# Start-up loads of a two-layer squared-ReLU kernel: x on one DMA queue, bias and first weights on the other

## Chip, cores and metric

The kernel runs on one core of a Trainium2 chip. The metric is the device time of one execution in microseconds: the median of three runs before the change is 290.73 us (290.58 to 290.94).

## What is computed

The reference is a dense layer, a squared ReLU and a second dense layer, all in bf16. x is 2048 rows of 576, the hidden width is 4608:

```python
h = jnp.einsum("bsd,df->bsf", x, w1) + b1
r = jnp.where(h > zero, h, zero)
h = r * r
out = jnp.einsum("bsf,fd->bsd", h, w2) + b2
```

## The kernel before

The 2048 rows are worked in four blocks of 512. For each block the first layer gives the hidden activations transposed (hidden column on the partition, row along the free dimension) in 36 groups of 128 hidden columns, the tile hT; the second layer then contracts over those groups. TensorE does the matmuls of both layers (L181, L183, L196, L198, L202 and L217 for the first, L253 and L272 for the second). ScalarE adds the bias and applies the ReLU as it reads a result out of PSUM (L169), VectorE squares it (L170).

Since 576 is four and a half times 128, the first layer has two forms. The first four groups of hidden columns (G = 4) use weights in full height: the tile w1n holds four chunks of 128 input rows by 512 columns, and w1n8 the last 64 input rows, once in each half of the partitions. The other 32 groups (`a_rows`) run as two matmuls of 64 rows side by side in the array, with weights from w1_h. These need each slice of the transposed x in both halves of the partitions, which VectorE makes with two copies, `dup_windows` (L115, L116).

**Blocks 1 to 3** of x are transposed by DMA (`load_xT`, on SyncE's queue). **Block 0**, with which the change has to do, is transposed on TensorE, and its start goes like this:

- Six matmuls of 512 columns and one of 256 on a constant keep TensorE busy first (WARM, L61 to L63).
- x comes in four tiles of 128 rows (`load_x`, L72; 144 KB each), w1n in four chunks (`load_w1n`, L76; 128 KB each). SyncE issues x tiles 0 and 2 and then w1 chunks 0 and 2; ScalarE issues x tiles 1 and 3 and then w1 chunks 1 and 3.
- ScalarE then runs a dummy activation (L97), ahead of which its table is loaded, and issues the load of the first bias into b1_rows (L98, 9 KB), a tile that VectorE clears first (L86). SyncE goes on with the two w1n8 loads (L79), fourteen w1_h loads (L82), the DMA transposes and all the rest.
- `a_full(0, "k_outer")` (from L213 on) issues, in this order on TensorE: the transposes of tiles 0 and 1, those of tiles 2 and 3 (five for each tile, L146), then for each chunk k four matmuls over the first 256 rows (`part(0, k)`, L217), four of chunk 0 over the other 256 rows, the transpose of the bias (L159), the twelve left of the other 256 rows, and the four 64-row matmuls with w1n8 (`pair`, L196 and L198). After those comes `a_rows` (L181, L183).
- `x_copies` brings the transposes out of PSUM for each half of the rows: VectorE copies three of the five slices (L151, L153), ScalarE two (L152). `dup_windows(0)` comes after both halves.

The order on each engine is that of the program for everything under `keep`. The loads all pass through two queues, SyncE's and ScalarE's; a load that waits holds whatever stands behind it on the engine that issues it.

Of the kernel before, what the change touches and what calls it, by code (L numbers as in the profile page):

```python
# [17 lines left out]
def kernel(  # L18
# [9 lines left out]
    nc = tc.nc  # L28
    keep = tc.keep_in_program_order
    P = 128  # L30
# [5 lines left out]
    NFT = F // P  # L36
    NC = D // H
    NK = NC // 2
# [6 lines left out]
    RT = SB // P  # L45
# [12 lines left out]

    wps = ps_h.tile([P, 512], FP32, name="wps", tag="ph")
    ones = nc.const_aps.tensor(1.0, [P, 512], BF16)  # L60
    WARM = [512] * 6 + [256]  # L61
    for i, n in enumerate(WARM):
        keep(nc.tensor.matmul(wps[:, 0:n], lhsT=ones[:, 0:P], rhs=ones[:, 0:n], start=True, stop=True))  # L63

# [6 lines left out]
    def load_x(eng, rt):  # L71
        keep(eng.dma_start(out=xs[:, rt, :], in_=x2[rt * P:(rt + 1) * P, :]))  # L72

    def load_w1n(eng, k0, k1):
        src = w1[k0 * P:k1 * P, 0:GW].rearrange("(k p) f -> p k f", p=P)
        keep(eng.dma_start(out=w1n[:, k0:k1, :], in_=src))  # L76
# [8 lines left out]
    b1_rows = const.tile([P, P], BF16, name="b1_rows")  # L85
    nc.vector.memset(b1_rows[:], 0.0)  # L86
    load_x(nc.sync, 0)
    load_x(nc.scalar, 1)
    load_x(nc.sync, 2)
    load_x(nc.scalar, 3)  # L90
    for k in range(NK):
        load_w1n(nc.sync if k % 2 == 0 else nc.scalar, k, k + 1)

    ident = const.tile([P, P], BF16, name="ident")
    make_identity(nc, ident[:])
    warm = const.tile([P, 1], FP32, name="warm")
    keep(nc.scalar.activation(out=warm[:], in_=nc.const_aps.tensor(0.0, [P, 1], FP32), func=ACT.Relu))  # L97
    keep(nc.scalar.dma_start(out=b1_rows[0:NFT, :], in_=b1.rearrange("(ft p) -> ft p", p=P)))  # L98
    for h in range(2):
        load_w1n8(nc.sync, h)  # L100

# [242 lines left out]
```

## Time and profile before

| what | value |
|---|---|
| median of three runs | 290.73 us |
| the profiled execution, its own time | 290.52 us |
| its span, first to last instruction | 288.7 us |
| TensorE busy in the span | 284.6 us (99%) |
| ScalarE, VectorE busy | 96.5 us, 78.6 us |
| first transpose of x on TensorE | 3.76 us |
| first matmul of the first layer (L217) | 5.41 us |
| first matmul of `a_rows` (L181) | 9.50 us |
| first of SyncE's and ScalarE's loads issued | 0.73 us |

Times inside the span count from its first instruction. The profiled execution is one run; 1.8 us of its own time lie around the span. PE is TensorE, PEld its weight loads, DVE VectorE, ACT ScalarE, POOL GpSimd, SP SyncE; ACTq and SPq are the parts of these engines that issue DMAs. A DMA is issued, moves its bytes as packets on 16 DMA engines that all queues share, and lands when its semaphore is complete. In the tables of groups, waits and chains a line such as L72 is the line of the kernel that issued the work, and what stands behind an arrow is what released a waiting engine.

### The profile page before, as it was taken

The numbers are of one execution on the slowest core, as the hardware profiler recorded it, in microseconds if no ns is written. First come the engines' busy times: TensorE is split into PE (matmuls) and PEld (weight loads), VectorE is DVE, ScalarE is ACT, GpSimd is POOL, SyncE is SP. The second block draws the span as 40 slices with busy tenths as digits, with TensorE's granted clock in tenths as the row PEclk, the third lists the DMA queues.
The fourth block names the chain that finished last, engine by engine and source line by source line (L and its number), as shares of the span: only waits on it lengthen the run. The fifth ranks groups of instructions, "written<-read, shape, count | busy, mean of one in ns | idle before, by whom it ended". The sixth has DMA issues, their size and how long they took to land.

```text
span 288.7 us, 4690 instructions
## 1 busy us (share of the span) xinstructions
PE 284.6 (99%) x2027; PEld 138.9 (48%) x2032; DVE 78.6 (27%) x177; ACT 96.5 (33%) x152; POOL 0.9 (0%) x7
## 2 busy tenths in 40 slices
PE   8999999999999999999999999999999999999996
PEld 5544444444444555555544444444444455555555
DVE  3444544444500200000025444444440001100001
ACT  3666666666500000000027666666670000000000
POOL 0000000000000000000000000000000000000000
PEclk9999999999999999999999999999999999999999
DMA  6999999600001100000000000000000110000000
GB/s 198 236 244 197 265 388 246 94 0 2 0 18 36 37 16 18 16 16 18 16 16 2 1 2 0 2 0 2 0 2 0 36 39 16 16 16 19 32 17 18
DMA packets 31573, 16.59 MB, mean 57 GB/s; under 512 B 15552, under 2 KB 31552, under 8 KB 31552
## 3 DMA queue, kind: packets, MB, share of 16 engines
q1 hardware_dynamic: 30928, 15.72, 22.3%
q10 hardware_dynamic: 624, 0.57, 0.7%
q8 instruction: 16, 0.26, 0.4%
q14 instruction: 5, 0.04, 0.0%
HBM read 11.43 MB, written 2.36 MB: 48 GB/s over the span
## 4 chain that ended last, share of the span: by engine, by line
PE 97%; DMA 1%; SPq 0%; issue 0%; DVE 0%
PE ph L181 42%; PE po L272 38%; PE pt L253 11%; PE pn L202 4%; DMA w1n<-in_w_dram 1%; PE pn L217 1%; PE ph L183 1%; PE pn L196 1%; SPq L72 0%; DVE o_sb L274 0%; PE b1T_ps L159 0%; PE pn L198 0%
## 5 line engine op out<-in xcount | busy, mean ns | idle before, releaser
L181 PE MATMUL ph<-xTw,w_h 64*128 64x512 bf16 x576 | 124.6, 376 | 0.0
L183 PE MATMUL ph<-xTw,w_h 64*128 64x512 bf16 x576 | 124.6, 376 | 0.0
L272 PE MATMUL po<-w_sb,hT 128*128 128x448 bf16 (+2 forms) x612 | 109.4, 341 | 0.0
L169 ACT ACTIVATE r<-ph,b1T 128x512 bf16<-128x512 f32 x128 | 81.1, 685 | 41.6 <-PE ph L183 41.6
L181 PEld LDWEIGHTS <-w_h 64*128 64x128 bf16 x576 | 54.1, 94 | 68.3
L272 PEld LDWEIGHTS <-hT 128*128 128x128 bf16 x612 | 58.5, 98 | 51.0
L170 DVE TENSOR_TENSOR hT<-r 128x512 bf16<-128x512 bf16 x144 | 61.2, 426 | 76.9 <-ACT r L169 76.9
L183 PEld LDWEIGHTS <-w_h 64*128 64x128 bf16 x576 | 54.1, 94 | 0.0
L274 DVE TENSOR_TENSOR o_sb<-po,b_bc 128x448 bf16<-128x448 f32 (+2 forms) x17 | 10.2, 597 | 125.8 <-PE po L272 125.8
L253 PE MATMUL pt<-hT,w_sb 128*128 128x512 bf16 x142 | 31.3, 379 | 0.1
L169 ACT ACTIVATE r<-pn,b1T 128x512 bf16<-128x512 f32 x16 | 10.3, 688 | 62.0 <-PE pn L198 60.6
L253 PEld LDWEIGHTS <-w_sb 128*128 128x128 bf16 x144 | 14.1, 98 | 17.0
L256 ACT ACTIVATE oT<-pt,b2T 128x512 bf16<-128x512 f32 x4 | 2.7, 687 | 28.3 <-PE pt L253 28.3
L202 PE MATMUL pn<-xTw,w1n 128*128 128x512 bf16 x45 | 10.4, 379 | 0.4 <-issue 0.3
L202 PEld LDWEIGHTS <-w1n 128*128 128x128 bf16 x48 | 4.5, 98 | 6.0 <-issue 0.8
L217 PE MATMUL pn<-xTw,w1n 128*128 128x256 bf16 x32 | 3.7, 273 | 0.1
L63 PE MATMUL wps<-const-bfloat16-1.0 128*128 128x512 bf16 (+1 forms) x7 | 2.9, 597 | 0.8 <-PEq L328 0.8
L217 PEld LDWEIGHTS <-w1n 128*128 128x128 bf16 x32 | 3.0, 98 | 0.6 <-DMA w1n<-in_w_dram 0.3
L115 DVE COPY xTw<-xTw 64x2048 bf16<-64x2048 bf16 x4 | 2.8, 690 | 0.6 <-ACT xTw L152 0.5
L116 DVE COPY xTw<-xTw 64x2048 bf16<-64x2048 bf16 x4 | 2.8, 688 | 0.1
L196 PE MATMUL pn<-xTw,w1n 64*128 64x512 bf16 x8 | 2.4, 379 | 0.0
L198 PE MATMUL pn<-xTw,w1n 64*128 64x512 bf16 x8 | 2.4, 379 | 0.0
(21 smaller groups left out, 10.5 us busy)
## 6 DMA issues: line engine op xcount, KB each, us to landing
w_sb<-in_w_dram SPq DMA_DIRECT2D x2, 2592.0 KB, 15.2
w_h<-in_w_dram SPq DMA_DIRECT2D x14, 288.0 KB, 6.6
out_dram<-o_sb SPq DMA_DIRECT2D x15, 112.0 KB, 1.7
w_h<-in_w_dram SPq DMA_DIRECT2D x4, 144.0 KB, 3.2
out_dram<-ot SPq DMA_DIRECT2D x4, 128.0 KB, 2.0
x_sb<-in_x_dram ACTq DMA_DIRECT2D x2, 144.0 KB, 3.0
x_sb<-in_x_dram SPq DMA_DIRECT2D x2, 144.0 KB, 3.0
w1n<-in_w_dram ACTq DMA_DIRECT2D x2, 128.0 KB, 3.6
```

Of the source, the lines that this page charges most:

```text
L63: keep(nc.tensor.matmul(wps[:, 0:n], lhsT=ones[:, 0:P], rhs=ones[:, 0:n], start=True, stop=True))
L115: keep(nc.vector.tensor_copy(out=xT[0:H, SPC:SPC + 4, :], in_=xT[H:P, E3:E3 + 4, :]))
L169: keep(nc.scalar.activation(out=r[:], in_=bank[:], func=ACT.Relu, bias=b1T[:, ft:ft + 1], scale=1.0))
L170: keep(nc.vector.tensor_tensor(out=hTs[sb][:, ft, :], in0=r[:], in1=r[:], op=ALU.mult))
L181: keep(nc.tensor.matmul(bx[:], lhsT=w1_h[0:H, LO_C[i], jc], rhs=xT[0:H, LO_W[i], :], start=(i == 0), stop=(i == NC - 1)))
L183: keep(nc.tensor.matmul(by[:], lhsT=w1_h[H:P, UP_C[i], jc], rhs=xT[H:P, UP_W[i], :], start=(i == 0), stop=(i == NC - 1)))
L196: keep(nc.tensor.matmul(banks[2 * i][:], lhsT=w1n8[0:H, 2 * i * P:(2 * i + 1) * P], rhs=xT[0:H, SPC, :], start=start, stop=stop, skip_grou ...
L202: keep(nc.tensor.matmul(banks[g][:], lhsT=w1n[:, k, g * P:(g + 1) * P], rhs=xT[:, O + k, :], start=start, stop=stop))
L217: keep(nc.tensor.matmul(banks[g][:, hc], lhsT=w1n[:, k, g * P:(g + 1) * P], rhs=xT[:, O + k, hc], start=(h == 0 and k == 0), stop=False, s ...
L253: keep(nc.tensor.matmul(pt[:], lhsT=w2_sb[:, ft, DM:D], rhs=hT[:, ft, :], start=(i == 0), stop=(i == NFT - 1)))
L272: keep(nc.tensor.matmul(po[:, 0:d1 - d0], lhsT=hT[:, ft, jj * P:(jj + 1) * P], rhs=w2_sb[:, ft, d0:d1], start=(i == 0), stop=(i == NFT - 1)))
L274: keep(nc.vector.tensor_tensor(out=o_sb[:, d0:d1], in0=po[:, 0:d1 - d0], in1=b2_bc[:, d0:d1], op=ALU.add))
```

## The change

The warm-up has one matmul of 512 columns less. SyncE issues all four x tiles, in order, ahead of its other loads. ScalarE issues the bias first, then the four w1 chunks, and then has the dummy activation. Nothing else is edited; SyncE's later loads follow the x tiles directly.

```diff
-    WARM = [512] * 6 + [256]
+    WARM = [512] * 5 + [256]
...
     load_x(nc.sync, 0)
-    load_x(nc.scalar, 1)
-    load_x(nc.sync, 2)
-    load_x(nc.scalar, 3)
-    for k in range(NK):
-        load_w1n(nc.sync if k % 2 == 0 else nc.scalar, k, k + 1)
+    keep(nc.scalar.dma_start(out=b1_rows[0:NFT, :], in_=b1.rearrange("(ft p) -> ft p", p=P)))
+    for rt in range(1, RT):
+        load_x(nc.sync, rt)
+        load_w1n(nc.scalar, rt - 1, rt)
+    load_w1n(nc.scalar, NK - 1, NK)
...
     keep(nc.scalar.activation(out=warm[:], in_=nc.const_aps.tensor(0.0, [P, 1], FP32), func=ACT.Relu))
-    keep(nc.scalar.dma_start(out=b1_rows[0:NFT, :], in_=b1.rearrange("(ft p) -> ft p", p=P)))
     for h in range(2):
         load_w1n8(nc.sync, h)
```

## The prediction

> **What bounds the kernel now.** First the page: engine shares and the chain of work that ended last.
>
> ```profile
> span 288.7 us, 4690 instructions
> PE 284.6 (99%) x2027; PEld 138.9 (48%) x2032; DVE 78.6 (27%) x177; ACT 96.5 (33%) x152; POOL 0.9 (0%) x7
> PE 97%; DMA 1%; SPq 0%; issue 0%; DVE 0%
> ```
>
> TensorE works without a pause from its first real matmul to the end, so an edit ahead of that matmul is worth just the shift of it. The chain in order of time (start, length, what), first 12 us, shows what that is:
>
> ```profile
> 0.73 0.40 SPq L72
> ...
> 1.20 0.44 SPq L72
> ...
> 1.68 3.68 DMA w1n<-in_w_dram
> 5.36 0.05 issue
> 5.41 2.36 PE pn L217 x20
> ```
>
> Call the start of the first L217 matmul T0: 5.41 us. It waits for w1 chunk 0, third on SyncE's queue (issued 1.68, landed 5.36). The timeline of weight loads shows what is ahead of it (start, busy, line, idle time before):
>
> ```profile
> 2.44 0.15 PEld L63 LDWEIGHTS <-const-bfloat16-1.0 128*128 128x128 bf16 x1 [0.27 <-issue]
> 2.86 0.15 PEld L63 LDWEIGHTS <-const-bfloat16-1.0 128*128 128x128 bf16 x1 [0.28 <-issue]
> 3.76 0.56 PEld L146 LDWEIGHTS <-x_sb 128*128 128x128 bf16 x10 [0.75 <-DMA x_sb<-in_x_dram]
> 4.55 0.56 PEld L146 LDWEIGHTS <-x_sb 128*128 128x128 bf16 x10 [0.23 <-DMA x_sb<-in_x_dram]
> 5.40 2.08 PEld L217 LDWEIGHTS <-w1n 128*128 128x128 bf16 x20 [0.29 <-DMA w1n<-in_w_dram]
> ```
>
> Ten transposes (tiles 0 and 1) start at 3.76, ten (2 and 3) at 4.55, done by 5.11; then 0.29 us idle. In program order all 20 stand ahead of T0. Last the windows (busy time of each engine, clock, DMA share, GB/s):
>
> ```profile
> 1.90:2.70 0.80, 0.80 (x3) 0.30 (x2) 0.00 (x0) 0.09 (x1) 0.00 (x0) 1.00 0.96 255
> 2.70:3.70 1.00, 1.00 (x3) 0.15 (x1) 0.00 (x0) 1.00 (x1) 0.00 (x0) 1.00 1.06 332
> 3.70:5.30 1.60, 1.47 (x21) 1.12 (x20) 0.77 (x4) 0.39 (x2) 0.00 (x0) 1.00 1.00 335
> ```
>
> The sixteen DMA engines are full from 1.9 to 5.3 us. T0 is set by how many bytes move ahead of the last thing that TensorE needs, whichever queue issues them.
>
> **What the skill says.** (1) DMA: Bandwidth & Descriptors, section Issuing engines are not separate DMA queues: both queues run on the same 16 engines. The trace agrees: 255 to 335 GB/s at a share of 1. (2) The same page, section Queues, rings and completion order: each engine goes round-robin between queues by packet. The packet records agree: while both queues are loaded, each starts about half the packets (3.0 to 5.0 us: 302 and 316). (3) TensorE: Matmul & The Clock Gate, section What's actually happening: the array is at half clock until it was busy for a free-running window of about 3.4 us. Agrees: warm-up loads are 427 ns apart for 512 columns, transposes 56 ns for 128, and the clock record grants full speed at 3.66 us for 286.72 us, 84 windows of 3.413.
>
> **Part 1, one warm-up matmul of 512 fewer.** Loads at 2.44 and 2.86 are 0.427 us apart, so TensorE is free at 3.28 rather than 3.71 us. By itself it saves nothing: tile 0 lands at 3.72. What it risks is the clock: the grant at 3.66 comes with TensorE busy for 2.9 of the 3.41 us before it; without the matmul and before any transpose it is 2.5. Whether that is enough the trace doesn't show; rival B prices it. Lower bound nothing.
>
> **Part 2, x alone on SyncE's queue, in order.** Landings here are an issue's start plus its time to landing in the DMA view. Today tiles 0 and 1 share the engines and land at 3.72 and 3.53, tiles 2 and 3 at 4.51 and 4.34. After: SyncE issues them 0.47 us apart (0.73 and 1.20 in the chain), at about 0.73, 1.20, 1.66, 2.13. First bytes move at 1.92, as today. ScalarE now issues the bias first; its bytes are nothing (9 KB), but its issue takes 0.70 us and waits for the memset (ends 0.94), so w1 chunk 0 is issued at about 1.71 and its bytes, 1.03 us later by ScalarE's first load of today, at 2.75. Until then x is alone: 0.84 us x 255 GB/s = 214 of 590 KB. The rest, 376 KB, shares with w1: a turn is 1152 against 1024 bytes, 53% of 334 GB/s = 177 GB/s, 2.12 us, to 4.87. From the last x packet today (4.05) to its landing (4.51) is 0.46 us, so tile 3 lands at about 5.33, 0.8 later than x is complete today. Check: 2.13 plus the 3.2 us that an x load of the second turn takes today is 5.33. Tiles 0 to 2 come at about 3.2, 3.8 and 4.6; their transposes are hidden under the wait for tile 3.
>
> After that landing come 0.04 us of release and five transposes, 0.28: T0 = 5.65, against 5.41: **+0.25 us**. The bounds: if x kept all the bandwidth that it is issued for, tile 3 lands 2.5 us after issue (the lowest lag of a load in this stage, a w1n8 one of 64 KB), at 4.6, and T0 is 4.95 (-0.45); if ScalarE's queue weighed as today, tile 3 lands like the fourth load of SyncE's queue today, 2.16 + 3.9 = 6.06, and T0 is 6.4 (+1.0). I take +0.25: the first ignores the full engines, the second ScalarE's later start, worth some 0.5 us of that.
>
> **Part 3, w1 chunks on ScalarE's queue.** Chunk 0: 131 KB at 157 GB/s from 2.75, landed near 4.1, 1.5 us ahead of use. Chunks 1 and 2, issued at 2.19 and 2.68, land near 5.0 and 5.8; used at T0 + 0.44 and T0 + 0.87 (20 matmuls take 2.18 us by load starts), 6.09 and 6.52. Chunk 3 is a ninth load, and the trace shows what a ninth does today:
>
> ```profile
> SPq L79 <- DMA x_sb<-in_x_dram: 0.9, 1, 0.9
> ```
>
> Eight semaphores are used in turn, and the ninth load waits until the first user of its semaphore has landed. Chunk 3 then goes out when tile 0 or the bias is in, 3.2 to 3.9 us, and lands near 6.2 to 6.9; needed at T0 + 1.31 = 6.96. Cost nothing, at the far end close to it.
>
> Queued behind that wait on ScalarE: the table load (1.28 us, today 2.61 to 3.89), the dummy activation (0.20) and the L152 copies, today 5.33 to 6.41, held up by the bias issue at 4.59. After: 3.2 + 0.45 + 1.28 + 0.20 puts L152 at 5.2 to 5.9; its first use is at 6.52 and it takes 0.59: hidden. The second copy ends near 6.5 to 7.1, the two window copies (1.4 us) at 7.9 to 8.5, and their user starts at T0 + 3.65 = 9.3: hidden. The bias is today transposed at 7.49 without a wait; earlier gains nothing.
>
> **Part 4, what SyncE issues next.** The two w1n8 loads and then 14 w1_h loads follow x on SyncE; today the first goes out at 3.54. Their wait becomes the bias's landing (near 3.2) or tile 1's (3.8): the stream shifts by -0.3 to +0.3 us. The tightest user today is the third row group: its load lands at 12.98, TensorE takes it at 13.18. With T0 0.25 later that slack is 0.4: no stall, but a gain over some 0.2 to 0.5 us would be given back there.
>
> **Sum.** 0 + 0.25 + 0 + 0. The profiled execution took 290.52 us, of which 1.8 lie around the span; 290.52 + 0.25 = 290.8. It is 0.21 under the median of the runs, 290.73, so on the median 291.0 (+0.09%). I count a change of 0.2% (0.58 us) as what a measurement of this kernel tells from none.
>
> **Rivals.** A, likeliest: as summed, 291.0, with 290.7 to 291.4 for the landing of tile 3 at 5.0 to 5.7.
>
> B, **the clock comes a window late**, the slower side. Place: the grant at 3.66. Price: it moves to 3.66 + 3.41 = 7.08; tile 3's five transposes take 107 rather than 56 ns (+0.26), and from T0 = 5.9 to 7.08 the L217 matmuls go at half speed, losing 0.6. With the 0.25: +1.1, 291.8. It decides if 2.5 us of warm-up with the transposes after it are too little for the window, or if transposes count for less than matmuls. For it: the busy part is cut from 85% to some 73%, and nothing shows the limit. Against: tile 0 lands at 3.2, so its five half-speed transposes fill 3.3 to 3.8 and the window to about 82%.
>
> C, **x gets through early**: the 4.95 of part 2, held by the third row group to about 0.4: 290.3. For it: x has a head start of 0.84 us. Against: full DMA engines.
>
> D, nothing moves: w1 chunk 0 would have to stay last. It lands near 4.1, so that needs tile 3 at 5.1; A's range has it.
>
> **Chances.** A 0.52, B 0.31, C 0.12, 0.05 for a later stream of w1_h loads or tile 3 at 6 us (291.5 and up). Slower by over 0.2% (above 291.3): B nearly whole, 0.29, a tenth of A, 0.05, and 0.05, together 0.39. Faster (under 290.15): 0.05 out of C. Same: 0.56. The range, 290.3 to 292.0, leaves out a third of C, the top of B and half of the last case, about 0.13; A's own is 290.7 to 291.4.
>
> **What would show it.** Right: the idle time before T0 is put down to x rather than w1; the last five L146 loads stand alone near 5.4; w1 chunk 0 lands a microsecond early; T0 is 5.5 to 5.8; later groups shift by the same amount. B shows as L217 loads twice as far apart as today's 109 ns, up to 7.1 us. C shows as T0 under 5.2 and a wait of L183 for a w1_h load. Wrong altogether: x3 landing under 4.8, or a wait for w1 chunk 3 or for L152 amid the L217 matmuls.

## The result, and the profile after

| | before | after |
|---|---|---|
| median of six runs, us | 290.67 (290.30 to 290.94) | 293.40 (291.66 to 293.93) |
| ratio, 95% interval | | 1.0087 (1.0060 to 1.0113) |
| the profiled execution, its own time and span, us | 290.52, 288.7 | 292.95, 291.2 |
| weight load of the first L217 matmul (L216 after), us | 5.40 | 6.60 |
| first matmul of `a_rows` in the chain, us | 9.67 | 12.08 |

The change makes the kernel 0.87% slower, some 2.5 us, where 0.25 us were predicted and 1.1 us in the worst rival. None of the versions that were run, with one of its edits or with several, came out faster than the kernel before. Lines after L98 stand one lower in the changed kernel: L145 is the transposes, L216 the first matmuls, L180 `a_rows`.

The page of the changed kernel, engine shares:

```profile
span 291.2 us, 4692 instructions
PE 286.6 (98%) x2031; PEld 140.2 (48%) x2031; DVE 78.5 (27%) x177; ACT 96.3 (33%) x152; POOL 0.9 (0%) x7
```

TensorE is busy 2.0 us more than before, with one warm-up matmul less to do, so a part of the loss is not idle time but slower work. The chain in order of time (start, length, what):

```profile
1.65 3.79 DMA x_sb<-in_x_dram
5.44 0.05 issue
5.49 1.42 PE tb L145 x10
6.91 3.27 PE pn L216 x20
10.18 0.06 PE b1T_ps L158
```

Before, the chain ran over w1 chunk 0 and its landing at 5.36. Now it runs over x tile 2, issued at 1.65 and landed at 5.44, and over the transposes of tiles 2 and 3. The first twenty L216 matmuls take 3.27 us; they took 2.36. The timeline of weight loads (start, busy, line, idle before) shows the rest:

```profile
3.01 1.07 PEld L145 LDWEIGHTS <-x_sb 128*128 128x128 bf16 x10 [0.43 <-DMA x_sb<-in_x_dram]
5.49 0.45 PEld L145 LDWEIGHTS <-x_sb 128*128 128x128 bf16 x5 [1.41 <-DMA x_sb<-in_x_dram]
6.19 0.45 PEld L145 LDWEIGHTS <-x_sb 128*128 128x128 bf16 x5 [0.26 <-DMA x_sb<-in_x_dram]
6.60 2.86 PEld L216 LDWEIGHTS <-w1n 128*128 128x128 bf16 x16
```

Tiles 0 and 1 come early, as was wanted (2.97 and 3.53). Tile 2 then lets TensorE idle from 4.08 to 5.49, and tile 3 comes at 6.15. The view ends at 9.4 us, and the sixteen L216 loads up to there take 2.86 us, where all twenty took 2.08: TensorE is still at half clock for most of them (the clock record grants full speed at 9.00). The windows of DMA traffic, in the stretches that the prediction used (the last two columns are the share of the DMA engines and GB/s):

```profile
1.90:2.70 0.80, 0.80 (x3) 0.30 (x2) 0.00 (x0) 0.00 (x0) 0.00 (x0) 1.00 0.96 287
2.70:3.70 1.00, 1.00 (x8) 0.66 (x7) 0.00 (x0) 0.21 (x1) 0.00 (x0) 1.00 0.89 196
3.70:5.30 1.60, 0.64 (x7) 0.38 (x4) 0.69 (x3) 1.59 (x3) 0.00 (x0) 1.00 0.96 310
```

Before it was 255, 332 and 335. The DMA engines move 196 GB/s from 2.7 to 3.7 us at a share of 0.89: they are held by slow packets, not out of work. In the packet records of that microsecond nine of 203 packets took 0.33 to 0.84 us, a third of all packet time, beside the usual 0.05; the kernel before has two such among 333.

The shift of 2.4 us adds up by steps. Tile 3's landing replaces chunk 0's as the last thing needed: 6.15 against 5.36, 0.79. Its transposes then lie on the path: five take 0.41 at half clock (6.19 to 6.60), 0.28 of it at any clock and 0.13 for the clock. From there to the transpose of the bias the loads take 3.31 us instead of 2.09, 1.22 for the clock. The sum is 2.42; the first `a_rows` matmul is 2.41 late.

### The profile page after: what moved, and what is told of

It is laid out like the page before. It is cut to its first block, busy times and chain, and to the rows that moved or that the text cites. A ratio compares the mean times of both kernels' runs of the same rounds, so it can differ in the third digit from the quotient of the medians.

```text
span 291.2 us, 4692 instructions
## 1 busy us (share of the span) xinstructions
PE 286.6 (98%) x2031; PEld 140.2 (48%) x2031; DVE 78.5 (27%) x177; ACT 96.3 (33%) x152; POOL 0.9 (0%) x7
## 3 DMA queue, kind: packets, MB, share of 16 engines
HBM read 11.43 MB, written 2.36 MB: 47 GB/s over the span
## 4 chain that ended last, share of the span: by engine, by line
PE 97%; DMA 1%; SPq 0%; DVE 0%; issue 0%
PE ph L180 42%; PE po L271 37%; PE pt L252 11%; PE pn L201 4%; PE pn L216 2%; DMA x_sb<-in_x_dram 1%; PE ph L182 1%; PE pn L195 1%; PE tb L145 0%; SPq L72 0%; DVE o_sb L273 0%; PE b1T_ps L158 0%; PE pn L197 0%
## 5 line engine op out<-in xcount | busy, mean ns | idle before, releaser
L180 PE MATMUL ph<-xTw,w_h 64*128 64x512 bf16 x576 | 124.6, 376 | 0.0
L180 PEld LDWEIGHTS <-w_h 64*128 64x128 bf16 x576 | 54.1, 94 | 68.3
L201 PEld LDWEIGHTS <-w1n 128*128 128x128 bf16 x48 | 4.5, 98 | 6.0 <-issue 0.8
L216 PE MATMUL pn<-xTw,w1n 128*128 128x256 bf16 x32 | 4.8, 322 | 0.0
L216 PEld LDWEIGHTS <-w1n 128*128 128x128 bf16 x32 | 3.7, 118 | 0.9
L145 PE MATMUL tb<-ident,x_sb 128*128 128x128 bf16 x20 | 2.7, 311 | 1.1 <-DMA x_sb<-in_x_dram 1.1
L145 PEld LDWEIGHTS <-x_sb 128*128 128x128 bf16 x20 | 1.9, 139 | 2.1 <-DMA x_sb<-in_x_dram 2.1
```

Source lines behind the costliest of these rows:

```text
L145: keep(nc.tensor.transpose(tb[h][bank][:, slot, q * P:(q + 1) * P], xs[:, j, c0:c0 + P], ident[:]))
L180: keep(nc.tensor.matmul(bx[:], lhsT=w1_h[0:H, LO_C[i], jc], rhs=xT[0:H, LO_W[i], :], start=(i == 0), stop=(i == NC - 1)))
L201: keep(nc.tensor.matmul(banks[g][:], lhsT=w1n[:, k, g * P:(g + 1) * P], rhs=xT[:, O + k, :], start=start, stop=stop))
L216: keep(nc.tensor.matmul(banks[g][:, hc], lhsT=w1n[:, k, g * P:(g + 1) * P], rhs=xT[:, O + k, hc], start=(h == 0 and k == 0), stop=False, s ...
```

## The experiments

Each run is compared with the kernel before on the same chip; a ratio is given with its 95% interval. Each also has one profile, and a landing or a rate read from it is one sample: in three profiles below with the same loads (changed kernel, old warm-up, hole filled) tile 3 lands at 6.15, 6.53 and 6.88.

### The clock

Theory L puts the whole loss down to the loads: x tile 3 lands late, and nothing else is lost. Two theories add a late clock for the slower L216 matmuls: W, the missing warm-up matmul makes it late; H, the hole on TensorE between the transposes of tile 1 and tile 2 does, with any warm-up.

**The short warm-up alone**, on the kernel before:

```diff
-    WARM = [512] * 6 + [256]
+    WARM = [512] * 5 + [256]
```

> The kernel before with one warm-up matmul of 512 less, its loads unchanged. Theory L (loads: the time comes from x tile 3 landing later because it shares the DMA engines with w1): no change, 290.7. Theory W (the shorter warm-up itself makes the full clock come late): slower, 291.5 to 292.5, with L217 loads twice as far apart for a while. Theory H (the clock is late because TensorE idles between the transposes of tile 1 and tile 2): the hole here is some 0.5 us between 3.3 and 3.8 only, so 290.7 to 291.0.

Measured: 291.07, ratio 1.0001 (0.9992 to 1.0010).

```profile
3.62 1.83 PEld L146 LDWEIGHTS <-x_sb 128*128 128x128 bf16 x20 [1.03 <-DMA x_sb<-in_x_dram]
5.40 2.12 PEld L217 LDWEIGHTS <-w1n 128*128 128x128 bf16 x20
```

All twenty transposes run without a hole between them, partly at half clock (the grant comes at 5.15). They end after w1 chunk 0 has landed (5.24), so the matmuls follow without idle time, at 5.40 as before and at full clock. W falls for this kernel.

**The new loads with the old warm-up**: the changed kernel with WARM as before.

```diff
-    WARM = [512] * 5 + [256]
+    WARM = [512] * 6 + [256]
```

> The changed kernel with the old warm-up (six of 512 and one of 256): the new loads alone. L: tile 3 lands near 6.1 again, first L217 matmul at 6.4 to 6.6, +1.1, and 291.8 if the clock comes in time. W: the clock comes in time, 291.8. H: the warm-up ends at 3.7, the transposes of tiles 0 and 1 at 4.8, a hole of 0.7 us is left before tile 2, so the clock is still late in a part of the runs: 292.3 to 293.2.

Measured: 293.44, ratio 1.0070 (1.0051 to 1.0090). Tile 3 lands at 6.53, the clock record grants full speed at 9.65. The new loads alone make most of the loss. Whether the missing warm-up matmul adds to it (1.0087 with it) can't be told, since the two intervals overlap. H, which asks for a hole (here 1.21 us), stands.

**The hole filled**, on the changed kernel:

```diff
                 for j in range(2):
                     x_transpose(j)
+                for _ in range(3):
+                    keep(nc.tensor.matmul(fill[:], lhsT=ones[:, 0:P], rhs=ones[:, 0:512], start=True, stop=True))
                 x_copies(0)
```

> The changed kernel with three matmuls of 512 on the constant between the transposes of tile 1 and those of tile 2, where TensorE idled from 4.0 to 5.5; the warm-up stays short. They are 1.28 us at half clock, 0.65 at full. L: 291.8 (tile 3 is as late as before, nothing else is lost). H: the clock comes within one window, so what was lost to it goes: 291.6 to 292.2, and the runs lie closer together. W: the clock is as late as in the changed kernel, 293.0 to 293.5.

Measured: 292.13 (291.84 to 292.34), ratio 1.0037 (1.0025 to 1.0049). The weight loads of its profile:

```profile
3.00 1.08 PEld L146 LDWEIGHTS <-x_sb 128*128 128x128 bf16 x10 [0.42 <-DMA x_sb<-in_x_dram]
4.04 0.25 PEld L224 LDWEIGHTS <-const-bfloat16-1.0 128*128 128x128 bf16 x2
4.57 0.15 PEld L224 LDWEIGHTS <-const-bfloat16-1.0 128*128 128x128 bf16 x1 [0.28 <-issue]
5.95 0.45 PEld L146 LDWEIGHTS <-x_sb 128*128 128x128 bf16 x5 [1.24 <-DMA x_sb<-in_x_dram]
6.93 0.28 PEld L146 LDWEIGHTS <-x_sb 128*128 128x128 bf16 x5 [0.52 <-DMA x_sb<-in_x_dram]
7.17 2.12 PEld L217 LDWEIGHTS <-w1n 128*128 128x128 bf16 x20
```

x is even later here than in the changed kernel (tile 3 lands at 6.88), but the grant comes at 6.63 and the twenty L217 loads take 2.12. Three matmuls that compute nothing win back over half of the loss: 1.0087 against 1.0037 of their own baselines, some 1.4 us. That part is the clock's, through the hole. The rest, 0.37% or 1.1 us, goes with the loads. It fits that two of the six runs with the old warm-up lie at 292.13 and 292.21, where the filled kernel is, and the other four at 293.44 to 293.79.

**A hole without new loads**: on the kernel before.

```diff
-    WARM = [512] * 6 + [256]
+    WARM = [512] * 2
```

> The kernel before with two warm-up matmuls instead of seven, so that TensorE idles from 1.8 to 3.5 us; loads unchanged, x lands at 3.7 to 4.5 and w1 chunk 0 at 5.3. It measures the clock alone. H (full clock comes only at the end of a window in which TensorE was busy for more than some three quarters): the clock comes between 6 and 8.5 us instead of 3.4 to 5.2, the first L217 matmul starts at 5.4 to 5.7, and the time is 0.5 to 1.2 us over the kernel before, 291.3 to 292.0. If the clock has no part in it: 290.8.

Measured: 291.74 (291.15 to 292.64), ratio 1.0030 (1.0020 to 1.0039). Its weight loads:

```profile
3.50 2.05 PEld L146 LDWEIGHTS <-x_sb 128*128 128x128 bf16 x20 [2.61 <-DMA x_sb<-in_x_dram]
5.50 3.11 PEld L217 LDWEIGHTS <-w1n 128*128 128x128 bf16 x20
```

The matmuls start 0.10 late and then take 1.03 us longer (3.11 against 2.08); the grant is at 7.53. With x and w1 landing as before, the late clock alone costs 0.9 us.

The records give the rule behind it. Full speed lasts a whole number of spans of 3.413 us in every profile that has the record (84 in the one before, 83 in the one after), so grants fall on a grid; its place against the kernel's start differs between executions (the grid passes 0.25 us before, 2.17 after). In the changed kernel the spans ahead of the grant were:

```profile
2.17:5.59 3.42, 2.27 (x16) 1.29 (x14) 0.69 (x3) 1.96 (x3) 0.00 (x0) 1.00 0.96 284
5.59:9.00 3.41, 3.41 (x21) 2.52 (x21) 2.06 (x5) 0.58 (x1) 0.00 (x0) 1.00 0.70 178
```

A span with TensorE busy for 2.27 us brought no grant, the next one, full, did. Over these profiles, every span that ended in a grant had 2.65 us or more busy, and the spans before them that brought none had up to 2.79 (with the bias last, below). The two overlap, so the busy time of the profile doesn't sort them alone. If there is one limit, it lies near four fifths of the span; that transposes count for less would explain the overlap (the 2.65 us, with w1 chunks 1 and 3 held back, are all warm-up, the 2.79 in part transposes), but it was not tested.

### The loads

Theory S was sharing of the DMA engines between x and w1, theory B a slow stretch made by the early bias. Both had to be changed on the way.

**One queue, in order**, on the changed kernel:

```diff
     for rt in range(1, RT):
         load_x(nc.sync, rt)
-        load_w1n(nc.scalar, rt - 1, rt)
-    load_w1n(nc.scalar, NK - 1, NK)
+    for k in range(NK):
+        load_w1n(nc.sync, k, k + 1)
```

> The changed kernel with the four w1 chunks on SyncE's queue behind the four x tiles; ScalarE issues the bias alone. L: x shares with nothing, tile 3 lands near 4.3 and w1 chunk 0 near 4.9, so the first L217 matmul is at 4.7 to 5.1, earlier than before; TensorE has no long hole and the clock is in time. But SyncE issues its w1n8 and w1_h loads some 1 us later than before, so L182 waits for w1_h: 290.6 to 291.6. If x is late for another reason than sharing (the bias ahead, or the order), tile 3 lands at 5.5 or later and the time is 292 to 293.

Measured: 291.38, ratio 1.0017 (1.0010 to 1.0023). Tile 3 lands at 4.90 and chunk 0 at 5.54; the matmuls start at 5.58. x without a rival lands 1.2 us earlier than in the changed kernel, which speaks for S, but 0.6 us later than the 4.3 expected. One queue alone moves less than two did before (321 and 334 GB/s in these two microseconds):

```profile
2.80:3.80 1.00, 1.00 (x9) 0.69 (x8) 0.00 (x0) 0.29 (x2) 0.00 (x0) 1.00 0.87 216
3.80:4.80 1.00, 0.79 (x9) 0.52 (x7) 0.63 (x3) 0.42 (x1) 0.00 (x0) 1.00 1.00 282
```

The expected wait for w1_h isn't seen; what waits is L216, for the chunks themselves.

**The bias last**, on the changed kernel:

```diff
-    keep(nc.scalar.dma_start(out=b1_rows[0:NFT, :], in_=b1.rearrange("(ft p) -> ft p", p=P)))
...
     keep(nc.scalar.activation(out=warm[:], in_=nc.const_aps.tensor(0.0, [P, 1], FP32), func=ACT.Relu))
+    keep(nc.scalar.dma_start(out=b1_rows[0:NFT, :], in_=b1.rearrange("(ft p) -> ft p", p=P)))
```

> The changed kernel with the bias load put back behind the dummy activation; x on SyncE's queue, w1 on ScalarE's, short warm-up. Theory S (sharing: x tile 3 is late because each queue gets half of the DMA engines): w1 chunk 0 now starts with x, 1 us earlier than in the changed kernel, so x shares from the start and tile 3 lands at 5.5 to 6.2; 292.0 to 293.5. Theory B (the early bias load is what slows the transfers between 2.8 and 4.3 us, where the changed kernel moves 138 to 254 GB/s and the one before 290 to 330): the rate in that stretch is back at 290 or more, tile 3 lands at 5.3 or earlier, and the time is 291.0 to 292.0.

Measured: 293.19, ratio 1.0079 (1.0056 to 1.0101). The rate is back, 365 and 348 GB/s in the two windows of 1 us from 2.8 on, and yet tile 3 lands at 6.45, since w1 shares from the first byte. The slow stretch and sharing are two things, and sharing from the first byte is enough for a late tile 3.

**The bias first**, on the kernel before (its load moved ahead of ScalarE's x tile 1):

```diff
     load_x(nc.sync, 0)
+    keep(nc.scalar.dma_start(out=b1_rows[0:NFT, :], in_=b1.rearrange("(ft p) -> ft p", p=P)))
     load_x(nc.scalar, 1)
...
-    keep(nc.scalar.dma_start(out=b1_rows[0:NFT, :], in_=b1.rearrange("(ft p) -> ft p", p=P)))
```

> The kernel before with the bias load put first on ScalarE's queue, ahead of x tiles 1 and 3; nothing else changed. B: the rate between 2.8 and 4.3 us falls to 140 to 260 GB/s here too, x tiles land over 1 us later, 292 or more. S: the rate stays near 300; x tiles 1 and 3 come 0.7 us later for ScalarE's later issue, x lands by 4.7 and w1 chunk 0 by 5.3, so 290.7 to 291.2.

Measured: 291.94 (290.92 to 293.57), ratio 1.0046 (1.0025 to 1.0066). The profile, of the slowest of the eleven runs, has 239 GB/s from 2.8 to 4.8 where the kernel before has 327; tile 3 lands at 6.53. The order "bias first" hurts without any of the other edits. B seemed shown.

**Two kernels that hold w1 back behind the table load.** The first is the changed kernel with all four w1 loads moved behind the dummy activation, the second the kernel before with chunks 1 and 3 there, ahead of the bias.

```diff
-        load_w1n(nc.scalar, rt - 1, rt)
-    load_w1n(nc.scalar, NK - 1, NK)
...
     keep(nc.scalar.activation(out=warm[:], in_=nc.const_aps.tensor(0.0, [P, 1], FP32), func=ACT.Relu))
+    for k in range(NK):
+        load_w1n(nc.scalar, k, k + 1)
```

```diff
-    for k in range(NK):
-        load_w1n(nc.sync if k % 2 == 0 else nc.scalar, k, k + 1)
+    for k in (0, 2):
+        load_w1n(nc.sync, k, k + 1)
...
     keep(nc.scalar.activation(out=warm[:], in_=nc.const_aps.tensor(0.0, [P, 1], FP32), func=ACT.Relu))
+    for k in (1, 3):
+        load_w1n(nc.scalar, k, k + 1)
```

> The changed kernel with the four w1 chunks put behind ScalarE's table load and dummy activation, so that they are issued some 1.4 us later and x has the DMA engines nearly to itself; bias first, short warm-up. S: tile 3 lands at 4.3 to 4.9 as in the run with one queue in order; the first L217 matmul waits for w1 chunk 0 instead, at 5.1 to 5.6; clock in time; 290.6 to 291.2. B: the slow stretch is still there and tile 3 lands at 5.5 or later; 292 or more.

> The kernel before with ScalarE's two w1 chunks (1 and 3) and its bias put behind its table load and dummy activation; x split over both queues, long warm-up. w1 chunk 0 is then alone behind x and lands at 4.8 to 5.0 instead of 5.36, so the first L217 matmul waits for the transposes, at 5.1; SyncE's w1n8 and w1_h loads come earlier too. By S 0.2 to 0.3 faster than the kernel before, 290.5 to 290.7; if chunk 1 comes too late for its use or the clock goes late, 290.9 to 291.2.

Measured: 292.41, ratio 1.0058 (1.0046 to 1.0071), and 291.03, ratio 1.0004 (0.9997 to 1.0011). Neither did what it was made for: the table load didn't hold ScalarE's next DMA, and the first chunk was issued at 1.68 and 1.73 while the table was loading. In the first kernel the other three were then held, one by one, by the semaphores of x tiles 0 to 2 (issued at 2.94, 3.99 and 4.99), and ScalarE's first copy behind them started at 5.37; it is the cost that the prediction feared for chunk 3 and that the changed kernel, whose chunk 3 goes out at 3.10, doesn't have. Tile 3 lands at 5.24 there, and the last first-layer matmuls of block 0 wait for the last w1 chunk, landed at 8.79. The second kernel has 365 GB/s from 2.8 to 4.3 us, without gain in time.

**The bias second**, between x tiles 1 and 3, on the kernel before:

```diff
     load_x(nc.scalar, 1)
+    keep(nc.scalar.dma_start(out=b1_rows[0:NFT, :], in_=b1.rearrange("(ft p) -> ft p", p=P)))
     load_x(nc.sync, 2)
```

> The kernel before with the bias load second on ScalarE's queue, between x tiles 1 and 3: both queues start at once as before, but the bias is still early. Theory B1 (the early bias load itself makes the transfers slow): between 2.8 and 4.3 us the rate falls to 140 to 280 GB/s and packets of over 250 ns are many, x tile 3 lands at 5.5 or later, 291.5 or more. Theory B2 (what is slow is a start with one queue only, because ScalarE's first large load goes out 0.9 us later; the bias is only its cause): the rate stays at 290 or more; x tile 3 comes 0.6 us later for its later issue, at 4.9, ahead of w1 chunk 0: 290.8 to 291.2.

Measured: 291.58, ratio 1.0032 (1.0018 to 1.0046). The slow stretch is there, half a microsecond later (204, 146 and 233 GB/s in the three half microseconds from 3.3 on). That was taken for B1, the bias's own transfer as the cause, against B2, a start in which one queue issues alone. But here, too, ScalarE's large loads have a break: x tile 3 goes out at 1.86.

**A late w1 without an early bias**, on the changed kernel with the bias last:

```diff
+    keep(nc.gpsimd.memset(w1n[:, 0, :], 0.0))
     load_x(nc.sync, 0)
```

> The changed kernel with the bias load behind the dummy activation, and GpSimd clearing w1 chunk 0's tile first, so that ScalarE's first load goes out some 0.8 us after SyncE's, about as in the changed kernel, without a bias load ahead of it. B1: no slow stretch, the rate from 2.8 to 4.3 us is at 290 or more, and x tile 3, which shares with w1 from 2.6 on, lands at 5.2 to 5.6 as the prediction worked out; 291.2 to 292.5 with the clock. B2: the slow stretch is there, tile 3 lands at 6 or later, 293.

Measured: 292.17 (290.84 to 293.38), ratio 1.0036 (1.0024 to 1.0048). The memset was shorter than meant and ScalarE's first load goes out at 1.29; 286 GB/s from 2.8 to 4.3, tile 3 at 6.10. The time spreads over 2.5 us, as a late clock makes it, so it tells little.

**Sharing alone**: the same with two memsets, and the hole filled as above.

```diff
+    for _ in range(2):
+        keep(nc.gpsimd.memset(w1n[:, 0, :], 0.0))
     load_x(nc.sync, 0)
-    keep(nc.scalar.dma_start(out=b1_rows[0:NFT, :], in_=b1.rearrange("(ft p) -> ft p", p=P)))
...
     keep(nc.scalar.activation(out=warm[:], in_=nc.const_aps.tensor(0.0, [P, 1], FP32), func=ACT.Relu))
+    keep(nc.scalar.dma_start(out=b1_rows[0:NFT, :], in_=b1.rearrange("(ft p) -> ft p", p=P)))
...
                     x_transpose(j)
+                for _ in range(3):
+                    keep(nc.tensor.matmul(fill[:], lhsT=ones[:, 0:P], rhs=ones[:, 0:512], start=True, stop=True))
```

> The changed kernel with the bias load behind the dummy activation, ScalarE's first w1 load held to about 1.7 us by two memsets of its tile on GpSimd (where it stands in the changed kernel), and three matmuls of 512 on the constant in TensorE's hole. No slow stretch from the bias, no late clock: what is left is sharing. As predicted (53% of the bandwidth for x): tile 3 lands at 5.2 to 5.5, first L217 matmul at 5.6, 291.0 to 291.4. If sharing alone makes the loss: tile 3 at 6.1 or later and 292.0, as with the hole filled and the bias early (292.13).

Measured: 291.55 (291.30 to 291.66), ratio 1.0020 (1.0011 to 1.0028), a little over the expected time. Tile 3 lands at 5.49, where the prediction's sum has 5.33, but the filling outlasts tile 2's landing and the matmuls start at 6.29.

**The same with the long warm-up instead of the filling** (the three filling matmuls are taken out again):

```diff
-    WARM = [512] * 5 + [256]
+    WARM = [512] * 6 + [256]
```

> The loads of the run with sharing alone (bias last, ScalarE's first w1 load held to about 1.8 us by two memsets on GpSimd), without the filling matmuls and with the long warm-up, which lasts to 3.7 and is followed by the transposes of tiles 0 and 1 to 4.8. If sharing costs what the prediction worked out, tile 3 lands at 5.2 to 5.6 and the first L217 matmul starts at 5.5 to 6.0: 291.1 to 291.4 against 290.85 before. If its cost was hidden by the filling and is larger, tile 3 lands at 6 or later: 291.8 or more.

Measured: 291.30 (291.04 to 293.36), ratio 1.0023 (1.0007 to 1.0040), in the range expected for sharing as predicted, while tile 3's landing is near the other one. The profile holds a surprise:

```profile
2.80:3.80 1.00, 1.00 (x6) 0.59 (x5) 0.00 (x0) 0.00 (x0) 0.00 (x0) 1.00 0.89 196
3.80:4.80 1.00, 0.59 (x10) 0.41 (x7) 0.49 (x3) 0.84 (x1) 0.00 (x0) 1.00 0.96 334
```

The slow stretch is there at 196 GB/s, as in the changed kernel, and the bias load is nowhere near (issued at 5.81); until 3.3 us SyncE's queue moves alone. Tile 3 lands at 5.99, half a microsecond later than with the same loads in the run before. So the stretch needs no bias load. And sharing without a slow stretch, at the changed kernel's point of start, was not isolated by any run.

This run also bears on the clock. TensorE has a hole of 1.33 us (4.21 to 5.54) behind the long warm-up, and only two of 13 runs lie 1.3 us or more above the rest (293.06 and 293.36, the others 291.04 to 291.75); the changed kernel with the old warm-up, with a hole of 1.21 us, had four of six high. The warm-up's length may thus matter where there is a hole; these runs are too few to say how much.

**What it is in the bias load.** Two kernels with the bias second: with 32 of its 36 rows there and four later, so that all 16 DMA engines get a share (12 completion packets end the 36 rows, 16 a large load), and with a load of the same shape out of x in the place of the bias (the bias itself is not loaded, so the output lacks it).

```diff
+    b1r = b1.rearrange("(ft p) -> ft p", p=P)
     load_x(nc.scalar, 1)
+    keep(nc.scalar.dma_start(out=b1_rows[0:32, :], in_=b1r[0:32, :]))
...
-    keep(nc.scalar.dma_start(out=b1_rows[0:NFT, :], in_=b1.rearrange("(ft p) -> ft p", p=P)))
+    keep(nc.scalar.dma_start(out=b1_rows[32:NFT, :], in_=b1r[32:NFT, :]))
```

```diff
     load_x(nc.scalar, 1)
+    keep(nc.scalar.dma_start(out=b1_rows[0:NFT, :], in_=x2[0:NFT, 0:P]))
...
-    keep(nc.scalar.dma_start(out=b1_rows[0:NFT, :], in_=b1.rearrange("(ft p) -> ft p", p=P)))
```

> The kernel before with 32 rows of the bias second on ScalarE's queue and the other four rows where the bias load was. If the uneven use of engines (36 rows go to 12 of 16) is what slows the transfers, there is no slow stretch now: 290 GB/s or more between 3.3 and 4.8 us, 290.8 to 291.2. If not, it is there as with the whole bias second (146 to 233 GB/s), 291.4 or more.

> The kernel before with a load of the bias's shape second on ScalarE's queue, but reading its 36 rows of 256 bytes out of x; the bias itself is left out, x values stand in for it. If the place that is read matters (another tensor, touched for the first time amid the x loads), there is no slow stretch: 290 GB/s or more between 3.3 and 4.8 us, 290.8 to 291.2. If it is the form of the load, the stretch is there, 291.4 or more.

Measured: 291.46, ratio 1.0029 (1.0013 to 1.0044), and 291.62, ratio 1.0031 (1.0019 to 1.0044). Neither number of engines nor source matters to the time. With 32 rows the profile is that of the fastest of ten runs: the issue takes 0.44 us instead of 0.66, the break is shorter, and only the window from 3.3 to 3.8 is slow (208 GB/s).

**Bias and break apart.** Two kernels, both from the one before. The first moves the bias load from ScalarE to GpSimd, early; the second leaves the bias and holds x tile 3:

```diff
+    keep(nc.gpsimd.dma_start(out=b1_rows[0:NFT, :], in_=b1.rearrange("(ft p) -> ft p", p=P)))
     load_x(nc.sync, 0)
```

```diff
+    for _ in range(2):
+        keep(nc.gpsimd.memset(xs[:, 3, :], 0.0))
     load_x(nc.sync, 0)
```

> The kernel before with the bias load issued early by GpSimd instead of ScalarE, so that both queues of the large loads run as before without a break. B1 (an early bias load slows the transfers): under 250 GB/s somewhere between 2.8 and 4.8 us, 291.3 or more. B2 (a break in the large loads of one queue does): 290 GB/s or more throughout, 290.6 to 291.0.

> The kernel before with x tile 3's load on ScalarE's queue held to about 1.8 us by two memsets of its tile on GpSimd; bias where it was. B1: no slow stretch; tile 3 lands at 4.9, 290.8 to 291.2. B2: a slow stretch as with the bias second (146 to 233 GB/s between 3.3 and 4.8 us), tile 3 at 5.5 or later, 291.4 to 291.8.

Measured: 291.10, ratio 1.0005 (0.9997 to 1.0014), and 292.05, ratio 1.0037 (1.0023 to 1.0051), more than B2 expected. First the windows of the early bias without a break, then those of the break without an early bias:

```profile
2.80:3.80 1.00, 1.00 (x6) 0.41 (x5) 0.00 (x0) 1.00 (x1) 0.00 (x0) 1.00 1.09 357
3.80:4.80 1.00, 1.00 (x13) 1.00 (x11) 0.18 (x1) 0.32 (x2) 0.00 (x0) 1.00 1.04 342
```

```profile
2.80:3.80 1.00, 1.00 (x7) 0.35 (x6) 0.00 (x0) 0.00 (x0) 0.00 (x0) 1.00 0.99 320
3.80:4.80 1.00, 0.81 (x15) 0.64 (x12) 0.54 (x3) 0.66 (x1) 0.00 (x0) 1.00 0.67 138
```

B2 holds: a break is enough, without an early bias. What hurts is that ScalarE's queue hands out no large load for half a microsecond or more while SyncE's does. That an early bias is harmless by itself is shown less well: GpSimd issued it at 1.41, and its bytes moved from 3.5 to 3.9 us, against 2.2 to 2.6 in the changed kernel. But with it early, the rates are no lower than with a break alone, so nothing is left for it to explain. All profiles, from the windows of 2.8 to 4.8 us; "break" is the longest time from 0.73 us on in which ScalarE's first three large loads have no issue under way:

| kernel | break, us | GB/s | tile 3 lands |
|---|---|---|---|
| before | none | 327 | 4.34 |
| short warm-up alone | none | 357 | 4.29 |
| early bias by GpSimd | none | 349 | 4.51 |
| two warm-up matmuls | none | 344 | 4.37 |
| w1 chunks 1 and 3 held back | 0.10 | 363 | 4.32 |
| bias last | none | 356 | 6.45 |
| changed | 0.89 | 240 | 6.15 |
| new loads, old warm-up | 0.88 | 249 | 6.53 |
| hole filled | 0.88 | 234 | 6.88 |
| bias first | 0.87 | 239 | 6.53 |
| bias second | 0.73 | 238 | 5.81 |
| 32 rows of bias second | 0.51 | 294 | 5.20 |
| shape of the bias, out of x | 0.72 | 257 | 5.85 |
| late w1, bias last | 0.56 | 296 | 6.10 |
| all four w1 chunks held back | 0.95 | 256 | 5.24 |
| sharing, filled | 1.17 | 293 | 5.49 |
| sharing, long warm-up | 1.17 | 265 | 5.99 |
| x tile 3 held | 0.86 | 229 | 6.09 |
| one queue in order | no large load | 249 | 4.90 |

A break that comes later is not in this column and isn't seen to hurt: with w1 chunks 1 and 3 held back, ScalarE issues nothing from 2.12 to 3.43 us, its queue still has bytes to move, and the rate is the highest of all.

## Why the prediction was wrong

**What bounds the kernel** was right: the chain still goes over one DMA to the first matmuls, and the shift at 12 us is the shift of the end (2.41 of the 2.43 us between the two profiled executions).

**Part 1** was right in the cost of the matmul (ratio 1.0001 alone) and right that the clock is what can be lost. It looked for the loss in the wrong place. It counted TensorE's busy time up to 3.66, as if the grid of grants stood still against the kernel; it doesn't.

**Part 2 failed**, in the term "2.12 us, to 4.87". Its first step was good: x is alone until 2.7 and tiles 0 and 1 land at 2.97 and 3.53 (3.2 and 3.8 predicted). Its last step was good as well: a release of 0.04 and five transposes. In between it took 334 GB/s from the profile before and gave x 53% of that. The profile before has that rate with both queues at work all the time; the change takes a queue out for 0.9 us, and then both together moved 196 GB/s in the microsecond that followed. The packet records of the changed kernel show which factor was wrong. From 2.75 to 4.75 us x had 51% of the bytes, so the share was right, but of 238 GB/s: 122 for x, not 177. In the last 0.9 us the total was back at 363 and x's part fell to a quarter, which the prediction didn't have either; why is not shown. The last x packet started at 5.67 instead of 4.87, and tile 3 landed at 6.15 instead of 5.33: a term of 2.12 us was in truth 2.9. The range of part 2, to 6.06, nearly held it, but I chose the middle, and "full DMA engines" was taken as a rate that stays.

The sentence that "Tiles 0 to 2 come at about 3.2, 3.8 and 4.6; their transposes are hidden under the wait for tile 3" is the other failed step. Tile 2 came at 5.44. The order that was to help, tile 0 and 1 early, takes TensorE's work forward and leaves 1.4 us of nothing behind it. In the kernel before, the four tiles land within 1 us, and the transposes leave only 0.23 us idle among them. I costed the waiting at nothing because something later sets the end; it is not nothing, for the clock counts it.

**Parts 3 and 4** held: chunk 3 was issued at 3.10, released by the bias's landing; L151, the window copies and w1_h cost nothing on the path. Chunk 0 landed at 5.26, not 4.1, still ahead of its use.

**Rival B** had the right mechanism at 0.31 and the wrong size: 0.26 + 0.6 for the clock, 7.08 for the grant. The grant came at 9.00, by the grid of that execution, and the clock cost 1.35 us in the profile and about 1.4 in the medians of the changed kernel and the one with the hole filled. It named the warm-up as the condition. The short warm-up without a hole loses nothing (1.0001), and filling the hole wins the clock's part back, so the hole between tiles 1 and 2 is what it takes; a warm-up of 0.43 us more doesn't close it (1.0070), though it may make a late grant rarer. The Trainium skill (TensorE: Matmul & The Clock Gate, What's actually happening) says that the window is free-running and doesn't reset at a kernel's start; I cited the section and then used 3.66 as a fixed time. The spans of 3.413 us agree with it, and so does the spread of the runs: 2.3 us for the changed kernel, 0.6 for the one before, whose TensorE has no such hole.

**Rival C** had it the wrong way round: the head start of x and the break in ScalarE's queue are the same thing.

That both terms were underestimated moved the result out of the range: with a landing 0.82 later and a clock of 1.35, the sum of 0.25 becomes 2.4.

What stays open: why a break in one queue slows both queues about a microsecond later. Over the profiles, the slow packets belong to x and to w1, and to either queue. How much sharing alone would cost at the changed kernel's start also stays open; with sharing from the first byte and no slow stretch tile 3 lands at 6.45, so it is not small. No version that was tried beats the kernel before.

## What to carry to other kernels

A rate read from a profile belongs to the pattern of issues that made it; when an edit changes which queues are at work at once, treat the rate itself as an unknown and give it a range. Bringing the first tile forward is worth nothing if the last one sets the start, and it can cost: price the hole that it opens on TensorE until the clock is granted, with the grant anywhere on a grid of 3.4 us. To see whether a loss is the clock's, fill the hole with matmuls that compute nothing and compare: here three filling matmuls told 1.4 us of clock from 1.1 us of loads.

## What the runs showed of the hardware

- Two queues that both issue large loads without a break of more than 0.1 us moved 327 to 363 GB/s between 2.8 and 4.8 us. With an early break of some 0.5 to 1.2 us in one of them it was 229 to 296 over the same stretch, down to 114 in the worst half microsecond (x tile 3 held, 3.8 to 4.3 us). The Trainium skill (DMA: Bandwidth & Descriptors, Issuing engines are not separate DMA queues) has it that issuing from several engines only saves issue time; at this start it did more: one queue in order moved 216 and 282 GB/s in the two microseconds in which two moved 345 and 369 (short warm-up alone; one profile each). Issue time isn't what held it: the one queue had issued all 590 KB of x by 2.56 us and had moved 474 KB by 3.8.
- A table load doesn't hold the DMA issues behind it in ScalarE's program: with the table loading from 1.62 to 2.90, a w1 load was issued at 1.68.
- Tile 0's load lands 2.2 us after its issue began when no other large load starts with it (changed kernel), and 3.0 when two x loads start together (kernel before).
- Eight semaphores serve the loads in turn, and a ninth load waits for the landing of the first: the changed kernel's first w1n8 load is issued at 2.98, behind the landing of x tile 0 at 2.97.
